# Three loads and one dummy matmul fewer at the start of a transformer block kernel

## Chip, cores and metric

One core of one Trainium2 chip. The time is device microseconds of one execution of the program; most executions of one kernel lie within 0.3% of each other. A profile gives one execution in detail; its span runs from the first to the last profiled instruction, and is a little shorter than the time. A run over 1.5% above the fastest of its kernel is called slow, any other fast.

## The reference, cut to what matters

A block of a diffusion transformer: two batches of 256 tokens, width 1152, two heads, hidden width 4608.

```python
mod = (silu(c) @ w_mod).reshape(B, 6, 1, D)          # shift_a, scale_a, gate_a, shift_m, scale_m, gate_m
h = layernorm(x) * (1 + scale_a) + shift_a
q, k, v = split(h @ wqkv)
a = softmax(q k^T * Dh**-0.5) v                      # two heads
x = x + gate_a * (a @ wo)
h2 = layernorm(x) * (1 + scale_m) + shift_m
return x + gate_m * (gelu(h2 @ w_fc1) @ w_fc2)
```

## The kernel before

The kernel writes its operations in one list; a small list scheduler orders them per engine and sets the semaphore waits. TensorE and SyncE keep the order of the list. SyncE does nothing but issue loads and stores (and wait for them). The loads at the start:

```python
for b in range(2):
    dma(X[:, 2 * b:2 * b + 2, :], xv[b], ...)                          # input, two halves
for (ka, kb) in ((0, KC), (KC, 2 * KC), (2 * KC, KT)):                 # KC = 3, KT = 9
    for k0, k1 in ((0, 3), (3, 6), (6, 9)):
        dma(WSC[:, k0:k1, ka * P:kb * P], ..., "ld_sc%d_%d" % (ka, k0))  # scale weights
    for kt in range(ka, kb):
        dma(WK[:, kt, :], wqkv_v[:, kt, D:2 * D], ..., "ld_wk%d" % kt)   # one K row (of 128 x 1152) each
        # the first one waits for the second half of the input
for k0 in range(0, KT, 3):
    dma(WSH[:, k0:k0 + 3, :], ..., "ld_sh%d" % k0)                       # shift weights, three loads
```

The start of TensorE's list, with the dummies (`warm`) that keep its clock up while it waits:

```python
def warm(n, tag, behind=None):          # n dummies of 512 columns into an unused bank, each after `behind`
    ...
warm(7, "b")
for n, behind in ((1, "bn_ln1_1_1"), (1, "aggr_ln1_1"), (2, "veps_ln1_1"), (1, "rstd_ln1_1")):
    warm(n, behind, behind)
xn_T(1)                                 # nine transposes of token tile 1
sca(0, 3)                               # scale columns: matmuls of 2 columns, wait for ld_sc0_0
warm(1, "d")
sca(3, 6)                               # ld_sc0_3
warm(1, "f", "bn_ln1_2_2")
xn_T(0, 0, 4)                           # first four transposes of token tile 0
sca(6, 9)                               # ld_sc0_6
xn_T(0, 4, 9)
hk(0, 0)                                # VectorE: first K input, scaled
...
k_first(0)                              # first K matmuls (256 columns): need hk(0, 0) and K row 0
...                                     # later: matmuls on the shift weights ("shr"), then the queries
```

## Time and profile before

| | before |
|---|---|
| time, three runs | 243.99 to 244.15 us, median 244.06 |
| span of the profiled run | 243.2 us (its time 244.43) |
| TensorE busy | 237.5 us, 98% |
| tile 1's transposes start, first K matmuls start | 8.34, 10.79 us |
| third shift load: landed, used | 28.97, 29.80 us |

A line of the timeline reads: start, length, engine, source line, operation, output<-input, count, and in brackets how long the engine was idle just before and what ended it. "SPq" is SyncE issuing. Here is the timeline's end, and three lines of the view of the DMA queues and issues (queue, packets, MB, share; issues with KB each and us from issue to landing):

```profile
240.52 1.07 SPq L669 DMA_DIRECT2D out_dram<-arena  x2
240.70 0.23 DVE L1299 TENSOR_TENSOR arena<-psum,arena 128x64 f32<-128x64 f32 x1 [0.21 <-PE psum L688]
240.96 0.22 DVE L1300 TENSOR_TENSOR arena<-arena 128x64 bf16<-128x64 f32 x1
```

```profile
q14 instruction: 4, 0.03, 0.0%
...
out_dram<-arena SPq DMA_DIRECT2D x1, 16.0 KB, 1.9
```

VectorE's last result is there at 241.18 us, and the store of it needs 1.9 us more. Queue 14 brings instructions, not data; four of its packets fall within the span.

### The profile page before, as it was taken

How to read it: one execution, taken by the hardware profiler on the slowest of the kernel's cores; microseconds unless marked ns; L12 is line 12 of the kernel's file. 1: busy time of each engine (PE TensorE's matmuls, PEld its weight loads, DVE VectorE, ACT ScalarE, POOL GpSimd, SP SyncE). 2: the span in 40 equal slices, each digit the busy share in tenths (PEclk: the TensorE clock that was granted, in tenths of full speed). 3: DMA queues.
4: the chain of work that ended last, by engine and by line, in shares of the span. 5: the costliest groups of instructions: out<-in, count | busy, mean ns of one | idle time of the engine just before them, and what ended most of it. 6: DMA issues, size and time to landing. Idle time of an engine off the chain costs nothing.

```text
span 243.2 us, 3996 instructions
## 1 busy us (share of the span) xinstructions
PE 237.5 (98%) x1717; PEld 145.8 (60%) x1726; DVE 120.1 (49%) x219; ACT 66.9 (28%) x136; POOL 21.5 (9%) x39
## 2 busy tenths in 40 slices
PE   7899999999999999999999999999999999999995
PEld 2588864556667666798444444444656566565664
DVE  2843388696988699789999500000022221111112
ACT  4820350354424107973233322222000000000000
POOL 1500000000021086500000000020000000000000
PEclk9999999999999999999999999999999999999999
DMA  6999999999996999989943498011000000000000
GB/s 231 333 363 388 390 392 392 395 414 405 392 353 190 346 392 392 392 277 393 323 161 85 150 324 307 0 31 70 0 16 19 16 16 19 16 16 21 28 19 18
DMA packets 31196, 51.58 MB, mean 212 GB/s; under 512 B 1479, under 2 KB 16843, under 8 KB 31179
## 3 DMA queue, kind: packets, MB, share of 16 engines
q1 hardware_dynamic: 30736, 50.14, 58.0%
q0 software_dynamic: 416, 1.19, 1.6%
q8 instruction: 13, 0.21, 0.4%
q14 instruction: 4, 0.03, 0.0%
q10 hardware_dynamic: 27, 0.00, 0.0%
HBM read 50.14 MB, written 1.19 MB: 211 GB/s over the span
## 4 chain that ended last, share of the span: by engine, by line
PE 95%; DVE 2%; DMA 2%; issue 0%
PE psum L688 93%; PE psum L691 2%; DMA arena<-in_x_dram 2%; DVE arena L741 1%; DVE arena L975 0%; DVE arena L762 0%; DVE arena L742 0%; DVE arena L1299 0%; DVE arena L1300 0%; DVE arena L966 0%; DVE arena L744 0%
## 5 line engine op out<-in xcount | busy, mean ns | idle before, releaser
L688 PE MATMUL psum<-arena 128*128 128x384 bf16 (+10 forms) x1628 | 234.1, 309 | 2.6 <-POOL arena L717 1.4
L688 PEld LDWEIGHTS psum<-arena 128*128 128x128 bf16 (+2 forms) x1637 | 140.7, 97 | 91.9 <-issue 3.2
L1091 DVE SCALAR_TENSOR_TENSOR arena<-arena 128x1152 f32<-128x1152 bf16 x32 | 44.7, 1414 | 0.6
L1299 DVE TENSOR_TENSOR arena<-psum,arena 128x384 f32<-128x384 f32 (+2 forms) x13 | 6.8, 526 | 68.3 <-PE psum L688 68.3
L1207 ACT ACTIVATE arena<-psum 128x512 bf16<-128x512 f32 (+1 forms) x44 | 22.5, 520 | 42.9 <-PE psum L688 42.7
L683 ACT ACTIVATE arena<-psum 128x512 bf16<-128x512 f32 (+6 forms) x38 | 19.9, 545 | 39.1 <-PE psum L688 37.1
L685 DVE CAST arena<-psum 128x512 bf16<-128x512 f32 (+3 forms) x13 | 8.1, 640 | 9.2 <-PE psum L688 9.2
L669 POOL DMA_DIRECT2D dit_scratch<-arena x3 | 1.8, 616 | 114.8 <-DVE arena L685 58.0
L1175 POOL TENSOR_TENSOR arena<-arena 128x384 f32<-128x384 f32 x12 | 10.9, 912 | 11.0 <-DVE arena L1174 9.8
L1118 DVE CAST arena<-psum 72x32 bf16<-72x32 f32 x1 | 0.2, 186 | 21.3 <-PE psum L688 21.3
L741 DVE BATCH_NORM_STATS2 arena<-arena 128x6 f32<-128x384 f32 (+1 forms) x18 | 9.5, 549 | 0.5 <-DMA arena<-in_x_dram 0.4
L1180 ACT ACTIVATE arena<-arena 128x1152 bf16<-128x1152 f32 x4 | 5.3, 1344 | 12.5 <-DVE arena L1179 12.5
L1174 DVE TENSOR_TENSOR arena<-psum,arena 128x384 f32<-128x384 f32 x12 | 6.4, 540 | 2.2 <-PE psum L688 2.1
L691 PE MATMUL psum<-arena 128*128 128x128 bf16 (+1 forms) x89 | 7.1, 219 | 0.4 <-DVE arena L762 0.4
L691 PEld LDWEIGHTS psum<-arena 128*128 128x128 bf16 (+1 forms) x89 | 5.7, 98 | 2.7 <-DMA arena<-in_c_dram 0.8
L1300 DVE TENSOR_TENSOR arena<-arena 128x384 bf16<-128x384 f32 (+2 forms) x13 | 6.8, 527 | 0.4
L1194 DVE TENSOR_SCALAR arena<-psum,arena 128x128 bf16<-128x128 bf16 x20 | 5.4, 334 | 1.8 <-PE psum L691 1.8
L1197 ACT ACTIVATE arena<-psum,arena 128x128 bf16<-128x128 bf16 x16 | 5.9, 464 | 0.6 <-PE psum L688 0.6
L1095 DVE STREAM_TRANSPOSE arena<-arena 128x1152 f32<-128x1152 f32 x4 | 5.5, 1370 | 0.0
L1098 DVE TENSOR_REDUCE arena<-arena 128x36 f32<-128x1152 f32 x4 | 5.4, 1346 | 0.0
L1021 ACT ACTIVATE arena<-psum,arena 128x256 bf16<-128x256 f32 x8 | 3.7, 472 | 1.3 <-PE psum L688 0.9
L807 DVE TENSOR_SCALAR arena<-arena,psum 128x256 bf16<-128x256 bf16 x2 | 0.6, 292 | 6.4 <-PE psum L688 6.4
(48 smaller groups left out, 48.3 us busy)
## 6 DMA issues: line engine op xcount, KB each, us to landing
arena<-in_w_fc_dram SPq DMA_DIRECT2D x9, 1152.0 KB, 7.0
arena<-in_w_fc_dram SPq DMA_DIRECT2D x4, 2592.0 KB, 17.3
arena<-in_w_mod_dram SPq DMA_DIRECT2D x18, 288.0 KB, 8.3
arena<-in_wqkv_dram SPq DMA_DIRECT2D x18, 288.0 KB, 8.3
arena<-in_w_mod_dram SPq DMA_DIRECT2D x3, 1728.0 KB, 20.5
arena<-in_w_mod_dram SPq DMA_DIRECT2D x3, 864.0 KB, 11.2
arena<-in_wqkv_dram SPq DMA_DIRECT2D x1, 2592.0 KB, 17.8
arena<-in_wo_dram SPq DMA_DIRECT2D x1, 2592.0 KB, 25.5
```

The lines of the kernel that those rows point to most:

```text
L683: act(c_act(n), lambda e: e.activation(out=dst, in_=src, func=ACTF.Copy), [src], [dst], name)
L685: dve(c_dve_psum16(n) if psum16 else c_dve_psum32(n), lambda e: e.tensor_copy(dst, src), [src], [dst], name)
L688: S.instr(lambda e: e.matmul(o, lhsT=l, rhs=r, start=st, stop=sp, **kw), reads=[l, r], writes=[o])
L691: S.instr(lambda e: e.transpose(o, i_, idn), reads=[i_, idn], writes=[o])
L741: dve(550, lambda e, s=s, o=o: e.bn_stats(out=o, in_=s), [s], [o], "bn_%s_%d" % (tag, ci))
L1091: dve(1270, lambda e, w=w, s=s, acc=acc: e.scalar_tensor_tensor(out=acc, in0=w, scalar=s, in1=acc, op0=ALU.mult, op1=ALU.add), [w, s, acc] ...
L1174: dve(550, lambda e, o=o, ga=ga, x1c=x1c: e.tensor_tensor(out=x1c, in0=o, in1=ga, op=ALU.mult), [o, ga], [x1c], "wo_t1_%d_%d" % (t, ci))
L1175: S.op("pool", 930, lambda e, xs=xs, x1c=x1c: e.tensor_tensor(out=x1c, in0=x1c, in1=xs, op=ALU.add), reads=[x1c, xs], writes=[x1c], name=" ...
L1197: act(440, lambda e, o=o, dst=dst, s1=s1, s2=s2: e.activation(out=dst, in_=o, func=ACTF.Identity, scale=s1, bias=s2), [o, s1, s2], [dst], ...
L1207: act(c_act(ntok), lambda e: e.activation(out=dst, in_=o, func=ACTF.Gelu_apprx_tanh), [o], [dst], "gelu_%d_%d" % (f, tok0))
L1299: dve(c_dve_psum32(w), lambda e, o=o, gm=gm, t1=t1: e.tensor_tensor(out=t1, in0=o, in1=gm, op=ALU.mult), [o, gm], [t1], "fc2_t1_%d_%d" % ( ...
L1300: dve(c_dve_32(w), lambda e, t1=t1, x1c=x1c, ost=ost: e.tensor_tensor(out=ost, in0=t1, in1=x1c, op=ALU.add), [t1, x1c], [ost], "fc2_out_%d ...
```

## The change

Its intent: less issuing on SyncE (K rows 7 and 8 in one load, the modulation rows in one instead of three), and one dummy less on TensorE's path.

```diff
-            for kt in range(ka, kb):
-                dma(WK[:, kt, :], wqkv_v[:, kt, D:2 * D], P * D * 2, "ld_wk%d" % kt, run=2304)
+            for kt in range(ka, kb - (kb == KT)):
+                k1 = KT if kt == KT - 2 else kt + 1
+                dma(WK[:, kt:k1, :], wqkv_v[:, kt:k1, D:2 * D], (k1 - kt) * P * D * 2, "ld_wk%d" % kt, run=2304)
...
-        warm(1, "f", "bn_ln1_2_2")
...
-        for k0 in range(0, KT, 3):
-            dma(WMODR[:, k0:k0 + 3, :], wmod_v[:, k0:k0 + 3, 2 * D:4 * D], 3 * P * 2 * D * 2, "ld_modr%d" % k0)
+        dma(WMODR, wmod_v[:, :, 2 * D:4 * D], KT * P * 2 * D * 2, "ld_modr")
```

## The prediction

> **What bounds the kernel now.** I read the page first (busy shares, slices, chain), then the chain in order of time, then the timeline of 9.5 to 10.9 us, where the removed matmul stands, and last each load's time from issue to landing. From the page:
>
> ```profile
> PE 237.5 (98%) x1717; PEld 145.8 (60%) x1726; DVE 120.1 (49%) x219; ACT 66.9 (28%) x136; POOL 21.5 (9%) x39
> DMA  6999999999996999989943498011000000000000
> GB/s 231 333 363 388 390 392 392 395 414 405 392 353 190 346 392 392 392 277 393 323 161 85 150 324 307 0 31 70 0 16 19 16 16 19 16 16 21 28 19 18
> PE 95%; DVE 2%; DMA 2%; issue 0%
> ```
>
> TensorE is busy 237.5 of 243.2 us and carries 95% of the chain that ended last. The DMA engines are full up to slice 11 (a slice is 6.08 us), so in the first 67 us two things are full at once. A load that falls away helps only where TensorE waits for a load, or where TensorE's own chain gets shorter. The chain, 8.3 to 13.7 us:
>
> ```profile
> 7.80 0.49 DVE arena L762
> 8.29 0.05 issue
> 8.34 0.68 PE psum L691 x9
> 9.01 0.91 PE psum L688 x20
> 9.92 0.22 PE psum L691 x4
> 10.14 0.21 PE psum L688 x9
> 10.36 0.30 PE psum L691 x5
> 10.66 0.13 issue
> 10.79 1.91 PE psum L688 x16
> 12.70 1.00 PE psum L691 x18
> ```
>
> Row four holds the two dummies of this place: 18 scale matmuls of 2 columns, the dummy "d" between them, and the dummy "f" last, ahead of tile 0's first four transposes. From 10.79 on the chain is TensorE almost without a break: in windows from 10.8 to 240.7 us its busy times add up to the window lengths less 0.7 us, and the longest hole among those is some 0.1 to 0.2 us once lost matmul records are discounted. So nearly all time won before 10.79 us should reach the end, provided no load becomes late. The timeline there:
>
> ```profile
> 9.36 0.56 PE L688 MATMUL psum<-arena 128*128 128x2 bf16 x8
> 9.76 0.38 PE L691 MATMUL psum<-arena 128*128 128x128 bf16 x4
> 9.98 0.38 PE L688 MATMUL psum<-arena 128*128 128x2 bf16 x9
> 10.22 0.44 PE L691 MATMUL psum<-arena 128*128 128x128 bf16 x5
> 10.29 0.62 DVE L807 TENSOR_SCALAR arena<-psum 128x256 bf16<-128x256 bf16 x2 [0.64 <-PE psum L688]
> 10.76 0.24 PEld L688 LDWEIGHTS psum<-arena 128*128 128x128 bf16 x3 [0.28 <-DMA arena<-in_wqkv_dram]
> 10.79 0.38 PE L688 MATMUL psum<-arena 128*128 128x256 bf16 x2
> ```
>
> The reader is to see two claims for the 0.13 us before 10.79. The weight load's bracket names the first K row (a DMA). But that row was issued at 6.36 us and took 4.1 us (the view of loads into that tensor, below), so it landed near 10.47; the VectorE scaling of the first K input began at 10.29, takes 0.35 to 0.36 us (view of its line), and so ended at 10.64. The later of the two is VectorE, and it waited 0.64 us for the small scale matmuls, that is for TensorE's own order. The dummy "f" is in that order.
>
> ```profile
> L669 SPq DMA_DIRECT2D arena<-in_wqkv_dram x1: 340/340/340, 6.4 to 6.4; - x1
> DMA to landing us min/median/max: 4.1/4.1/4.1
> ```
>
> **What the Trainium skill says.** "TensorE: Matmul & The Clock Gate", section "Wait — 56ns, not 53.3ns?": back-to-back matmuls of 512 columns start 426.7 ns apart cold and 215.7 ns warm. The trace agrees: the five dummies at 1.42 us take 2.31 us to the end of the last, which is four steps of 0.42 plus one latency of 0.63; four at 6.75 take 1.23 us with a latency of 0.38. So dummy "f" is warm and occupies about 0.216 us, not the 0.38 us that its row shows. The same page, "What's actually happening", says that the clock falls back to half after about 3.4 us of idleness; the hole that this change leaves is far shorter, and the granted clock is 1.00 in every window I asked for.
> "DMA: Bandwidth & Descriptors", section "Rules for kernel authors", advises joining small transfers and at least 1 MiB per DMA. The trace doesn't show a loss to be won back here: slices 5 to 7, where the 288 KB loads flow, move 392, 392 and 395 GB/s, and the neighbours that hold the 1728 KB loads 414 and 405. The section "Queues, rings and completion order" says that each engine consumes a queue's descriptors in ring order, so a joined load lands about when its last part landed.
>
> **The change part by part.**
> K rows 7 and 8 in one load. Removed: one issue on SyncE, 0.43 us (432 to 435 ns in the view of loads at 14.0 to 14.5 us). SyncE does no arithmetic and its queue is full by then: those two loads took 7.4 and 7.6 us to land (at 21.4 and 22.1 us), though 288 KB needs 0.75 us at 392 GB/s. Issuing later loads 0.43 us sooner only lengthens their queueing. The consumer uses both rows together, after the matmuls of row 6; those begin at 22.8 us and are 14 of 0.109 us, so about 24.3 us, over 2 us after the pair lands. Worth 0.
> Modulation rows in one load. Removed: two issues. The three occupy SyncE for 10.50 us (33.73 to 44.23), because the queue takes them no faster than memory delivers; one of 5184 KB would block it as long, and the next load (the output projection's weights) is issued near 44.2 us either way. Their landings are 20.5, 18.9 and 21.0 us after issue, about 54.3, 58.7 and 63.0 us. The matmuls that read them begin near 66.3 us; waiting for one landing at 63.0 instead of 54.3 still leaves 3.3 us. Worth 0.
> Dummy "f". Removed: 0.216 us of TensorE. The four transposes then start at about 9.55 instead of 9.76: their input was ready, its VectorE instruction having run from 8.73 to 9.31. The next scale matmuls go from 9.98 to 9.77; the last weights they need were issued near 2.88 us and landed at 9.62, 0.15 us before. VectorE's scaling goes from 10.29 to 10.07 and ends near 10.43; the K matmuls could start at 10.57 instead of 10.79. The first K row, landed at 10.47, needs some 0.05 to 0.1 us to be seen, so it allows a start near 10.55: just not the new bound, in this execution. ScalarE's copies, the VectorE variance of tile 3 and the GpSimd power behind it all follow the same transposes and shift along.
> Sum: 0 + 0 - 0.216, less a part for executions in which the K row or the scale weights land later. I take 0.18 us: 244.06 - 0.18 = 243.88 us.
>
> Does anything later eat it? Slack of loads against a TensorE that is 0.2 us earlier: the second K row lands at 11.15, used at 11.55 (0.2 left); the third shift load is issued at 17.02, lands 12.0 us later at 29.0, used at 29.8 (0.6 left); the last query row lands 10.7 us after 31.0, at 41.7, used at 43.4 (1.5 left); the value weights land 17.8 us after 32.2, at 50.0, used near 52.7. None turns into a wait.
>
> **The rivals.** (1) The first K row becomes the bound: the wait that replaces the one removed. For it: the bracket names it, and my margin is only some 0.1 us; its load itself waits for the second half of the input (2.7 us of SyncE waiting), which the change doesn't touch. Against: its landing is before VectorE's end. If it landed 0.15 us later in typical runs, the gain would be about 0.05: 244.0 us.
> (2) The loads do help: less issue time on SyncE brings everything forward, up to 0.43 us and more. Against: the DMA engines have no idle slice to fill, and TensorE never waits there. It would make about 243.4 us if it came on top.
> (3) The joined loads hurt: coarser landing delays the rows' matmuls. Against: 3.3 us and 2 us of slack. For it to show, the landing must slip by more than that; each further us would cost up to one: 244.5 or more.
> (4) The kernel is ordered by a list scheduler with modelled times; another model time for loads can swap neighbours on VectorE or ScalarE after about 31 us. Orders up to there are pinned in the code. Could move 0.3 us either way.
> (5) The clock falls to half for one window of about 3.4 us, because the dummy is gone: an estimate of 1.7 us, 245.6 us. Against: TensorE stays dense from 8.34 us with a hole of about 0.3 us, as before.
>
> **Range and chances.** The centre is 243.88. Three runs of before spread over 0.16 us, so the gain is about as large as that spread. Rival 1 pulls to 244.0, rivals 2 and 4 to 243.4 and 243.6, chip to chip noise both ways: 243.5 to 244.25 should hold 8 times in 10. Two per cent is 4.9 us; no rival reaches it. Faster by over 2%: 0.003; within 2%: 0.994; slower: 0.003.
>
> **What would show each step.** Right: the transposes of tile 0 start near 9.55 and the 16 first K matmuls near 10.57 to 10.6 us, in a span near 243.0; the merged K load lands near 22.1 and the merged modulation load near 63; no new wait of TensorE for a load. Rival 1: TensorE's hole before the first K matmuls grows from 0.35 towards 0.5 us between starts, and they still begin near 10.75. Rival 2: landings of the shift and query loads earlier by more than 0.2 us, and TensorE ahead by more than at 10.8 us. Rival 3: a wait for modulation weights at 66 us. The prediction is wrong if the start of the K matmuls moves by 0.2 us and the end does not, or if the end moves by more than 0.4 us.

## The result

The changed kernel: 243.82, 244.08, 244.40 us and one run of 356.75; before, in the same rounds, 243.92 to 244.15. Ratio of the fast runs 1.0003, 95% interval 0.9983 to 1.0022. (A ratio is the mean time of one kernel's fast runs over the mean of the other's of the same rounds, so not quite the ratio of the medians.) No change that these runs can see, and inside the predicted range.

The profile that came with it is of the run of 356.75 us. Three lines: from its page, its timeline at 50 us, and its transposes of token tile 1; the fourth shows the same transposes in the kernel before:

```profile
PE 351.5 (99%) x1725; PEld 180.1 (51%) x1725; DVE 121.2 (34%) x219; ACT 67.6 (19%) x136; POOL 21.5 (6%) x39
```

```profile
49.52 4.76 PE L688 MATMUL psum<-arena 128*128 128x512 bf16 x14
...
8.17 0.86 PE L691 MATMUL psum<-arena 128*128 128x128 bf16 x9
```

```profile
8.34 0.68 PE L691 MATMUL psum<-arena 128*128 128x128 bf16 x9 [0.36 <-DVE arena L762]
```

VectorE, ScalarE and GpSimd are as busy as ever (121.2, 67.6 and 21.5 us); TensorE alone is slow, 0.32 us per matmul of 512 columns instead of 0.216. The starts of single matmuls show since when. The dummies of the start are about 0.427 us apart at first in every trace. In the thirteen fast traces they are 0.216 apart from some point between 4.6 and 6.8 us on; in the slow one they are 0.287 and 0.360 apart in turn from 5.86 us on, as its later matmuls are, and the nine transposes of tile 1 take 0.86 us where every fast trace has 0.68. So the slow state was there over 3 us ahead of the place of the removed dummy (9.6 us in that trace) and further ahead of the joined loads: the change did not start it. The clock of 1.00 that is listed for this run says nothing: its trace holds no record of the granted clock (its page has no row PEclk), and 1.00 is what stands there then. I compare fast runs only, and ran the same kernel twice more.

The fast profile comes from the first of these reruns (its source lines are shifted by one against before). The chain of waits there:

```profile
7.90 0.68 PE psum L691 x9
8.58 0.67 PE psum L688 x19
9.25 0.24 PE psum L691 x4
9.49 0.21 PE psum L688 x9
9.71 0.30 PE psum L691 x5
10.01 0.13 issue
10.14 1.91 PE psum L688 x16
```

The timeline of the same place:

```profile
9.11 0.38 PE L691 MATMUL psum<-arena 128*128 128x128 bf16 x4
...
9.63 0.62 DVE L808 TENSOR_SCALAR arena<-psum 128x256 bf16<-128x256 bf16 x2 [0.43 <-PE psum L688]
```

The row before tile 0's transposes holds 19 matmuls for 20 and lasts 0.67 for 0.91 us. From tile 1's transposes to the first K matmuls it is now 2.233 us instead of 2.449: 0.216 less, to the nanosecond what the dummy occupies. Then, later, a wait that before did not have (view of waits from 27 to 31.5 us; engine, what it waited for, us in total, times, longest), and after it the issues and the tail (issues, queue):

```profile
PEld psum L688 <- DMA arena<-in_w_mod_dram: 0.4, 1, 0.4
```

```profile
q14 instruction: 3, 0.02, 0.0%
...
arena<-in_w_mod_dram SPq DMA_DIRECT2D x1, 5184.0 KB, 29.4
...
arena<-in_wqkv_dram SPq DMA_DIRECT2D x1, 576.0 KB, 8.6
...
out_dram<-arena SPq DMA_DIRECT2D x1, 16.0 KB, 1.4
```

Three things to see. TensorE waits for shift weights, so some of the 0.216 us is given back. The joined loads land where I expected (issued at 33.41 and 13.38, so at 62.8 and 22.0 us). And the last store takes 1.4 us instead of 1.9, while queue 14 has one packet less in the span. The span is indeed 242.1 to 242.7 us in the fast runs, half a microsecond or more below the 243.2 us of before's profiled run, though the time isn't lower: time minus span is 1.70 to 1.78 us, against 1.2 to 1.3 before. Half a microsecond left the span and came back behind it.

### The profile page after: what moved, and what is told of

It reads as the page before. It is cut to its first block, busy times and chain, and to the rows that moved or that the text cites. A ratio compares the mean times of both kernels' runs of the same rounds, so it can differ in the third digit from the quotient of the medians.

```text
span 355.0 us, 3999 instructions
## 1 busy us (share of the span) xinstructions
PE 351.5 (99%) x1725; PEld 180.1 (51%) x1725; DVE 121.2 (34%) x219; ACT 67.6 (19%) x136; POOL 21.5 (6%) x39
## 4 chain that ended last, share of the span: by engine, by line
PE 99%; POOL 0%; DVE 0%; issue 0%; POOLq 0%
PE psum L688 97%; PE psum L691 2%; POOL arena L714 0%; DVE arena L1298 0%; DVE arena L1299 0%; POOL arena L713 0%; POOL arena L718 0%; POOLq L1360 0%
## 5 line engine op out<-in xcount | busy, mean ns | idle before, releaser
L688 PE MATMUL psum<-arena 128*128 128x384 bf16 (+8 forms) x1636 | 346.2, 401 | 1.5 <-POOL arena L718 1.4
L688 PEld LDWEIGHTS psum<-arena 128*128 128x128 bf16 (+2 forms) x1636 | 173.2, 118 | 169.4 <-issue 71.9
L691 PE MATMUL psum<-arena 128*128 128x128 bf16 (+1 forms) x89 | 9.3, 263 | 0.0
L691 PEld LDWEIGHTS psum<-arena 128*128 128x128 bf16 (+1 forms) x89 | 7.5, 116 | 3.4 <-DMA arena<-in_c_dram 0.8
L1016 DVE TENSOR_REDUCE arena<-psum 128x2 f32<-128x512 f32 x4 | 2.8, 692 | 6.8 <-PE psum L688 6.8
## 6 DMA issues: line engine op xcount, KB each, us to landing
arena<-in_wqkv_dram SPq DMA_DIRECT2D x1, 2592.0 KB, 10.5
```

Source lines behind the costliest of these rows:

```text
L688: S.instr(lambda e: e.matmul(o, lhsT=l, rhs=r, start=st, stop=sp, **kw), reads=[l, r], writes=[o])
L691: S.instr(lambda e: e.transpose(o, i_, idn), reads=[i_, idn], writes=[o])
```

## The experiments

The theory from the prediction: the dummy's 0.216 us leave TensorE's chain, the loads give nothing. Its rivals: the first K row becomes the bound; fewer loads help; coarser loads hurt; another order on VectorE or ScalarE. The last fell without a run: compared instruction by instruction, the programs of before and after have the same order on VectorE, ScalarE and GpSimd. Each experiment was timed in five rounds against before on the same chip; "before" is 244.25 us in mean (11 runs) in the first group, 244.28 (11) in the second, 244.06 (9) in the third.

### e1_after_again, e8_after_third: the changed kernel again

No edit.

> The changed kernel once more, since the only profile of it fell into a run of 356.75 us. My theory (the dummy's 0.216 us comes off TensorE's chain, the loads give nothing): fast runs 0.1 to 0.2 us below the kernel before; in a fast profile tile 0's transposes start near 9.55 us and the first K matmuls at 10.57 to 10.60 us. Rival 1 (the first K row is the bound): K matmuls start at 10.70 or later, time 0 to 0.05 us below before. Rival 2 (fewer loads help): landings of the shift and query loads over 0.2 us earlier, time 0.4 us or more below. If the slow run belongs to the changed kernel (dummy missing, clock not held), some of its runs here are again near 350 us and none of the kernel before; if it is chance, it need not come back.

> The changed kernel a third time, for the size: 0.1 to 0.25 us below before, no run near 350 us. K matmuls 2.23 us after tile 1's transposes. The third shift load lands between 29.0 and 29.8 us; when it lands later than 21.5 us after tile 1's transposes, TensorE waits for it and some of the 0.216 us is given back.

Measured: mean 243.93 and 244.04 us, six fast runs each, ratios 0.9986 (0.9971 to 1.0001) and 0.9991 (0.9977 to 1.0006); medians 243.95 and 244.04. The gain is 0.32 and 0.24 us in means; in the first result there was none (fast means 244.10 against 244.03 us). No slow run among these twelve. The start of the K matmuls after tile 1's transposes is 2.233 and 2.235 us. Both traces wait 0.4 us at the third shift load, which landed 21.6 us after tile 1's transposes (29.45 and 29.80 us). From the first K to the first query matmul TensorE took 0.19 us more in each than in traces without that wait (22.47 against 22.28 us, and 22.27 against 22.08 in traces in which the record of the first query matmul is not lost): almost the whole 0.216.

### e2_only_dummy

```diff
-        warm(1, "f", "bn_ln1_2_2")
```

> The kernel before without dummy f; all loads as before. My theory: the same as the whole change, 0.1 to 0.2 us below before, K matmuls from 10.57 to 10.60 us. Rival 2: no gain or much less than with the loads joined. If the missing dummy causes slow runs, they show here too.

Measured: 244.13 us in mean, ratio 0.9994 (0.9981 to 1.0008). K matmuls at 2.232 us after tile 1's transposes. In this execution the third shift load landed 20.8 us after them and TensorE did not wait. The expected 0.1 to 0.2 us agrees with the measured 0.12, but the interval includes zero.

### e3_only_loads

The diff of the change without its line on `warm`.

> The joined loads alone, dummy f kept. My theory: 0.0 (within 0.1 us of before); joined K load lands near 22.1 us, joined modulation load near 63.0 us, projection weights near 69.7 us, first K matmuls at 10.79. Rival 2 (loads help): 0.2 us or more below before. Rival 3 (coarse landing hurts): 0.2 us or more above, with a wait of TensorE for a load.

Measured: 244.24 us, ratio 0.9999 (0.9984 to 1.0014): nothing, as expected, so neither rival 2 nor rival 3 shows in the time. The joined modulation load landed at 62.95, the projection weights at 69.7; the joined K load at 23.1, a microsecond later than expected and still in time. Yet the span is 0.5 us shorter in mean (242.50 against 243.00), with the time as before. So it is the loads, not the dummy, that move the half microsecond out of the span. This trace, with the dummy kept, waits 0.2 us at the third shift load too (landed at 29.82 us, 21.6 after tile 1's transposes), but loses nothing by it: the first query matmul comes 22.28 us after the first K matmul, as in before.

### e4_six_dummies

```diff
-        warm(1, "f", "bn_ln1_2_2")
+        warm(6, "f", "bn_ln1_2_2")
```

> The kernel before with six dummies f instead of one: 5 x 0.216 = 1.08 us more on TensorE ahead of tile 0's transposes. My theory: K matmuls start at 11.87 instead of 10.79 and the end comes 1.08 us later (245.1 us), since TensorE has no later wait that could absorb it. Rival (time at the start is absorbed later, by a wait for loads or for another engine): less than 0.8 us later at the end though 1.08 at the start.

Measured: 245.02 us, 0.77 above before, ratio 1.0031 (1.0017 to 1.0045). The K matmuls start 3.656 us after tile 1's transposes, so 1.207 later (1.08 for the dummies, the rest a wait for scale weights in that execution). The expected 1:1 fails. From the first query matmul to VectorE's last instruction this trace needs 207.66 us, before 208.12: 0.45 us less, most of it between 93 and 103 us. Before waits there (waits from 92 to 104 us):

```profile
PEld psum L688 <- DVE arena L1194: 0.5, 3, 0.2
PEld psum L691 <- ACT arena L1180: 0.3, 1, 0.3
```

The same view of this kernel has no such line. TensorE came later, so the engines that it used to wait for may have been done; but one trace doesn't show that this is the cause. The traces of e9 and e10 (below) have no such line either and need 207.66 and 207.73 us, with a TensorE that was earlier than before's. What is shown is that in six runs, all within 0.17 us, only 0.77 of at least 1.08 us reached the end. My statement that TensorE has no later wait was too strong. Those waits are short ones of 0.1 to 0.3 us, and I had looked for long ones.

### e5_no_d_no_f, e6_no_d_no_f_k0_early

```diff
-        warm(1, "d")
```

and for the second also

```diff
-                if kt == 0:
-                    S.instrs[-1].deps.update(j for j in S.instrs if j.name == "ld_x1")
```

> The changed kernel without dummy d as well: 0.216 us less again ahead of tile 0's transposes, in theory. My theory, with what the first runs showed: from the first transposes of tile 1 to the first K matmuls it was 2.449 us before and 2.233 without f. Without d the bound should change to the scale weights (third load, about 1.26 us after tile 1's transposes) and the first K row (landing 1.5 to 2.1 us after them, plus about 0.1): 2.05 to 2.2 us, so 0.03 to 0.18 gained there. At the end 0 to 0.1 us below the changed kernel, because the third shift load (landing at 29.0 to 29.8 us) then makes TensorE wait. Rival (the load stream has room): another full 0.2 us at the end.

> As the kernel without d and f, but the first K row is issued without SyncE waiting for the second half of the input, about 2.6 us sooner. If the first K row is the bound of the K matmuls there (rival 1), they now start at 2.02 us after tile 1's transposes; if the loads of input or scale weights are slowed by it instead, those land later and nothing is won. At the end no more than 0.1 us beyond the one before, as the bytes ahead of the third shift load are the same; if the whole load stream comes forward with it (by the gap that the wait leaves), the third shift load lands up to 1 us earlier and the end may gain 0.2 us.

Measured: 244.02 and 244.14 us, ratios 0.9993 (0.9976 to 1.001) and 0.9996 (0.998 to 1.0011). Without d the K matmuls start at 2.221 us, only 0.012 sooner than in the changed kernel. Timeline:

```profile
10.09 0.34 DVE L808 TENSOR_SCALAR arena<-psum 128x256 bf16<-128x256 bf16 x1
...
10.45 0.44 PEld L688 LDWEIGHTS psum<-arena 128*128 128x128 bf16 x5 [0.41 <-DMA arena<-in_wqkv_dram]
```

VectorE's scaling ends at 10.43 and the first K row landed at 10.41: both meet. With the row issued sooner it landed at 9.75, and the K matmuls started at 2.071 us, 0.15 earlier. So rival 1, the first K row, is the next bound, right behind the one removed. And it is worth nothing yet: in that trace the third shift load landed at 29.46 us, TensorE waited 0.5 us for it and lost 0.28. The bytes ahead of that load are the same in all these kernels.

### e7_14_more_loads

```diff
-        dma(WV, wqkv_v[:, :, 2 * D:3 * D], D * D * 2, "ld_wv", run=2304)
-        for k0 in range(0, KT, 3):
-            dma(WMODR[:, k0:k0 + 3, :], ...)
+        for k0 in range(KT):
+            dma(WV[:, k0:k0 + 1, :], wqkv_v[:, k0:k0 + 1, 2 * D:3 * D], P * D * 2, "ld_wv%d" % k0, run=2304)
+        for k0 in range(KT):
+            dma(WMODR[:, k0:k0 + 1, :], ...)
```

> The kernel before with 14 loads more: modulation rows in nine loads instead of three, value weights in nine instead of one. My theory: 0.0 (within 0.1 us of before), the last modulation load at 62.6 to 63.0 us, no new wait. Rival 2 (each load on SyncE costs time): 14 x 0.04 to 0.43 us, so 0.6 to 6 us later in those landings and up to that at the end.

Measured: 243.42 to 244.00 us in five runs and 245.21 in the sixth, mean 243.93, ratio 0.9987 (0.9965 to 1.0009), median 243.67. The run of 245.21 has no explanation. The other five are 0.6 us below before, and faster with more loads was in neither theory. (The last modulation load landed at 62.5 us, and TensorE did not wait for a load of weights after the first K row.) The tail tells why: the last store took 1.41 us, as in the kernels with fewer loads, but time minus span is 1.23, as in the kernel before. This kernel has the good half of each.

### A new theory: when SyncE fetches its program

The records of DMA packets hold the time of each packet of queue 14. Besides the packets ahead of the span and three of 8 KB that come near 28, 62 and 106 us in every fast trace, there is one late 8 KB packet, and its time moves with the number of instructions on SyncE:

| kernel | SyncE's instructions | late packet, us | last store, us | time minus span, us (mean) |
|---|---|---|---|---|
| before | 82 | 241.98 | 1.89 | 1.25 |
| e2_only_dummy | 82 | 241.43 | 1.81 | 1.26 |
| e4_six_dummies | 82 | 242.53 | 2.10 | 1.27 |
| e1_after_again | 79 | 243.17 (behind the span) | 1.41 | 1.73 |
| e3_only_loads | 79 | 243.58 (behind) | 1.41 | 1.74 |
| e8_after_third | 79 | 243.47 (behind) | 1.41 | 1.74 |
| e7_14_more_loads | 96 | 190.47 | 1.41 | 1.23 |

The Trainium skill, "Runtime: NRT & Kernel Launch", section "Instruction fetch mechanics", says that each engine's sequencer fetches the next block of its program by DMA while it runs the current one, and that the cost is mostly hidden. The theory: with 82 instructions SyncE's fetch falls into the last store and delays it; with 79 it falls behind the span and delays the end there; in the middle of the kernel it would cost nothing. (e5 and e6, with 79, are as e1: late packet behind the span, 1.41 and 1.73 to 1.74 us.) If so, the number of instructions counts, not the number of loads. Eight or three instructions that do nothing (an increment of a semaphore that nobody reads), placed behind the modulation load where SyncE has time, tell the two apart:

```diff
+                    if ins.name == "ld_wo":
+                        for _ in range(8):           # 3 in e11
+                            eng_handle.sem_inc(sems["pad"])
                     bi = ins.fn(eng_handle)
...
-            sems = {e: es.enter_context(nc.semaphore("c_" + e)) for e in ENGINES}
+            sems = {e: es.enter_context(nc.semaphore("c_" + e)) for e in ENGINES + ("pad",)}
```

### e9_after_8_incs, e10_before_8_incs, e11_after_3_incs, e12_only_dummy_8_incs

> The changed kernel with eight idle instructions more on SyncE (an increment of an unused semaphore) behind the modulation load. New theory: SyncE fetches its next 8 KB of program by DMA when it comes to about its 80th instruction; with the 82 of before this falls into the last store (241.98 us, store 0.5 us longer), with the 79 of the changed kernel behind the span (243.2 to 243.6 us, time minus span 1.75 instead of 1.25 us). With 87 it falls near 210 to 218 us, where nothing waits: last store lands 1.41 us after its issue, time minus span 1.25, so 0.5 us below the changed kernel and 0.7 to 0.8 below before. If it is the number of loads and not of instructions, it is as the changed kernel: 1.75, and 0.2 to 0.3 below before.

> The kernel before with the same eight idle instructions (90 on SyncE). Theory of the fetch: fetch near 195 to 205 us, last store 1.41 instead of 1.89 us, time minus span 1.25, so 0.5 us below before with all loads and dummies as before. If the joined loads were what shortened the span: as before, 1.8 to 2.1 us for the last store.

> The changed kernel with three idle instructions, so as many on SyncE as before (82), with three loads fewer. Theory of the fetch: the picture of before returns, with the fetch near 241 to 242 us, the last store 1.8 to 2.1 us, time minus span 1.25, and the same time as the changed kernel (0.2 to 0.3 below before, for the dummy). If the number of loads is what counts: 1.41 and 1.75 as in the changed kernel.

> Dummy f removed, all loads as before, eight idle instructions: as the joined loads with eight (0.7 to 0.8 us below before), within 0.1 us, if the joined loads are worth nothing by themselves. If their coarser landing costs something at the third shift load, this one is faster by 0.1 to 0.2; if they save something, slower.

| kernel | SyncE's instructions | late packet, us | last store, us | time minus span, us | mean time, us | ratio to before (95%) |
|---|---|---|---|---|---|---|
| e9_after_8_incs | 87 | 236.57 | 1.40 | 1.25 | 243.59 | 0.9980 (0.9968 to 0.9993) |
| e10_before_8_incs | 90 | 224.94 | 1.42 | 1.25 | 243.67 | 0.9984 (0.9971 to 0.9996) |
| e11_after_3_incs | 82 | 241.57 | 1.83 | 1.26 | 244.10 | 1.0001 (0.9989 to 1.0014) |
| e12_only_dummy_8_incs | 90 | 225.26 | 1.42 | 1.23 | 243.67 | 0.9983 (0.9970 to 0.9997) |

The changed kernel with three idle instructions has the tail of before again, with three loads fewer (its view of issues):

```profile
out_dram<-arena SPq DMA_DIRECT2D x1, 16.0 KB, 1.8
```

and the kernel before with eight has the short one, with all its loads:

```profile
out_dram<-arena SPq DMA_DIRECT2D x1, 16.0 KB, 1.4
```

So the number of SyncE's instructions decides, as the theory says, and the half microsecond is real time: 0.40 us in mean for the kernel before with eight instructions more (interval of the ratio: 0.1 to 0.7 us). Where I put the fetch was off (236.6 instead of 210 to 218, 224.9 instead of 195 to 205): I counted from the changed kernel for a threshold read off the kernel before. The sizes were missed as well: I expected e9 and e12 0.7 to 0.8 us below before, e10 0.5 and e11 0.2 to 0.3. Measured are 0.47 and 0.39 below, 0.40 below, and 0.03 above: e9, e11 and e12 held 0.2 to 0.3 us for the dummy, which did not show. That the packet is SyncE's is inferred from how it moves with SyncE's instructions and nothing else; no record names its engine. How it delays the store by half a microsecond is not shown.

For the dummy and the loads these four say: e12 against e10 (dummy alone, fetch out of the way in both) 0.01 us slower; e9 against e10 (dummy and loads) 0.07 us faster; e11 against before (same number of SyncE's instructions) 0.03 us slower. Against e9, e12 is 0.08 slower: no cost of coarser loads is seen. In e9 and e12 TensorE waits 0.4 and 0.5 us at the third shift load; in e10 and e11 it does not. e9, the changed kernel with its fetch moved, beats the kernel before by 0.2%. The changed kernel itself was not in these rounds; it had 0.9986 and 0.9991 to before, against e9's 0.9980, so a lead of e9 over it is likely but not shown.

## Why the prediction was right, and where its steps were not

The range held the result, and the centre of 243.88 us lies 0.2 below the median of the three fast runs (244.08) and near the means of the reruns (243.93 and 244.04).

- The dummy occupies 0.216 us and leaves the path to the first K matmuls: right, 2.449 to 2.233 us; the traces of e1, e2, e8, e9 and e11 lie at 2.232 to 2.235. (In e12 it was 2.341: there the input came early, and the K row, landed at 10.29, was the bound of a start at 10.34.) VectorE, not the K row that the bracket names, was the bound: right, since the start moved by the whole dummy.
- Rival 1 just short of taking over: right. One dummy more gave 0.012 us, and the row issued sooner 0.15.
- "None turns into a wait": this step failed. I gave the third shift load 0.6 us of room, from one trace. In the traces it lands between 20.6 and 21.8 us after tile 1's transposes, with the joined K load (20.7 to 21.6) as without (20.6 to 21.8), and the trace of before happens to be the earliest. In e1, e8 and e9 (the change) and e12 (the dummy alone) TensorE waited for it, losing 0.18 to 0.28 us; in e2 and e11 it did not. So the 0.18 at the end was probably too large as a mean. Six contrasts that contain the removal of f (e2 and e11 against before, e12 and e9 against e10, e1 against e3, e8 against before) give 0.12, -0.03, -0.01, 0.07, 0.31 and 0.24 us, mean 0.12; with the first result (-0.07) it is 0.09. They share runs, and the 95% intervals for such contrasts reach 0.3 us and more to either side. About 0.1 us, not clear of zero, is what can be said; that the result lay so near the centre is partly luck.
- The loads are worth 0: right in the time (e3, ratio 0.9999), and the landings were where I put them within 1 us. But my reason left out the tail. Three instructions fewer on SyncE shorten the last store by 0.5 us and lengthen the end behind the span by as much. That the two cancel was no part of my reasoning, so for the number it was luck; why they are of equal size is not shown. I had put the span near 243.0; it is 242.1 to 242.7. One step on the way was wrong without harm: the joined modulation load holds SyncE for 6.9 us in e1, not 10.5, and the projection weights are issued at 40.34 us, not near 44.2, yet land at 69.5 us, as before (69.7).
- Two readings in the text on the skill don't show what they are said to. The 1.23 us of the four dummies at 6.75 hold a wait of the last one, so they don't give a step of 0.216; the steps between 4.56 and 5.42 us of the same trace do. And slice 7 holds the value weights (2592 KB, landing at 50.0 us) and no load of 288 KB. Neither changes the forecast.
- Rival 2 (fewer issues help) fell in a way that I had not thought of: more instructions on SyncE help.
- The slow clock (rival 5) did not come. The one run of 356.75 us is much worse than its 245.6 and is not explained by it: that trace is slow from 5.86 us on, ahead of the place of the dummy. It came once in 16 runs of the changed kernel, and in none of the 35 runs of before and the 33 runs of the other kernels without f. Its cause stays open, and so does what the clock did there.

## What to carry to other kernels

A gain of a fraction of a microsecond at the start reaches the end only if every transfer that lands just in time has that much room in each execution, and one trace doesn't show the spread. Look at the tail too: the time from the last result to the end of the program can hold half a microsecond that belongs to no engine's work, and idle instructions on an issuing engine can move it away. When span and time move differently, ask what lies behind the last instruction. And when one run is far slower, look where in its trace the slowness begins: if that is ahead of the edit's place, the edit did not start it.

## What the Trainium skill lacked or had wrong

- "Runtime: NRT & Kernel Launch", section "Instruction fetch mechanics", calls the cost of a fetch mostly hidden and gives blocks of 16 KiB. In the middle of the kernel the runs agree. At the end it is not hidden: if the late packet is SyncE's, it costs 0.5 us in the last store (1.81 to 2.10 instead of 1.40 to 1.42 us) or behind the span (1.73 instead of 1.25 us), and 0.40 us of time came back when it was moved. The packet that moves with SyncE's instructions has 8 KB; those of the other instruction queue, q8, have 16 KB each.
- "TensorE: Matmul & The Clock Gate" has no state like that of the run of 356.75 us: matmuls of 512 columns 0.287 and 0.360 us apart in turn (0.216 in fast runs; the cold first dummies 0.427), from 5.86 us to the end. Its trace holds no record of the clock.
- No page that I read says how much the landing of one load varies between executions: the third shift load, 9.1 MB into the stream of loads, landed 20.6 to 21.8 us after the same instruction of TensorE in thirteen traces.
- "DMA: Bandwidth & Descriptors", section "Rules for kernel authors", advises large transfers. For loads of 288 KB and more in a full queue it made no difference here: three loads fewer 0.0 us (ratio 0.9999), fourteen more no slower (0.9987, interval 0.9965 to 1.0009).
